# Query scores as two column tiles of 64 and 60 tokens instead of one tile of 120

## The chip, the cores and the metric

The kernel runs on one core of one Trainium2 chip. The metric is the device time of one execution in microseconds (us). Engines: PE is TensorE's matmul, PEld its weight load, DVE VectorE, ACT ScalarE, POOL GpSimd, SP the queue that issues DMAs.

## The reference

Agent attention over 4 batches of 12480 tokens with 128 channels and 49 agents, followed by a feed-forward layer with 2048 hidden units whose activation is h * cos(h). All in float32.

```python
scale = 1 / sqrt(128)
def sm(a, b):                       # softmax over the last axis
    s = scale * (a @ b.transpose(0, 2, 1))
    e = exp(s - s.max(-1, keepdims=True))
    return e / (e.sum(-1, keepdims=True) + 1e-9)
agent_v = sm(agents, k) @ v         # 49 x 128 per batch
x = sm(q, agents) @ agent_v         # 12480 x 128 per batch
h = x @ w_in                        # 128 -> 2048
out = (h * cos(h)) @ w_out          # 2048 -> 128
```

## The kernel before

Tokens go in groups of 960 (GRP): 8 tiles (GT) of 120 tokens (TT), 13 groups a batch, 52 groups in all. The kernel folds `agent_v @ w_in` into one matrix `a` per batch, so that a group's hidden values come straight from its 49 softmax weights per token.

The main loop has 832 steps, 16 for a group: 2 chunks of 480 columns by 8 pairs of hidden blocks. In step n, `first_product` (L976) makes two matmuls into a PSUM tile `ph` (3 buffers), ACT takes the cosine (L979), DVE forms (cos - 1) * h (L985), and four steps later (LAG) `second_product` (L1001) multiplies by `w_out` into a small PSUM tile `one` (2 buffers, of which the output holds one); L997 and L998 add the remaining linear part once a chunk, and ACT copies the chunk out (L1008).

Between these steps stand the pieces that prepare later groups and later batches. They are set to steps by a plan written in the code (`plan`, `early_plan`, `extra`), and a scheduler sets the order of each engine's queue from the program order with a few instructions pinned:

- Query scores of a group (L157, or L167 for the first three groups): for each of the 8 tiles the 120 tokens are the stationary operand (128 channels x 120 tokens) and the 49 agents the moving one. The result has a token in each of 120 PSUM partitions and 8 x 49 columns. These are float32 matmuls, and each stands in the trace as two weight loads and two matmuls: 16 passes a group. ACT or DVE copies the scores to SBUF (L598, L653), DVE takes the maximum (L602), POOL subtracts it (L604).
- The exponentials are not taken group by group but in three windows of the run, in long ACT instructions (L665 for query groups, L497 for the next batch's agents), since ACT must change its table for them (ACT_TABLE_LOAD).
- Weights are normed by POOL (L689) into `p_in`, turned by four transposes (L698) into one PSUM tile, copied by ACT (L702), and split by POOL into `pT` (L705, L706).
- Agent scores of the next batch (L485, L487), their transposes (L505) and their products with the values (L521). L485/L487 and the two kinds of L521 (and L405/L406, L454 in the start-up) already write to partitions 0 to 63 and 64 to 112 of one PSUM tile, as two column tiles.

Before the main loop, a start-up of some 67 us prepares the first batch.

Of the kernel before, what the change touches and what calls it, by code (L numbers as in the profile page):

```python
# [9 lines left out]
F32 = mybir.dt.float32  # L10
# [33 lines left out]
def agent_attention_cos_ffn(ctx, tc, qT, kT, v, vk, vk_rest, agT, w_in, w_out, outT):  # L44
    nc = tc.nc
# [105 lines left out]
    def scores(sb, src, b, ps):  # L151
# [19 lines left out]
    class Weights:  # L171
# [372 lines left out]
    with ExitStack() as pools:  # L544
# [31 lines left out]
        PIECES = 7  # L576

        def piece_tiles(piece):
            e = sb.tile([TT, PIECES * GT, NA], F32, name="e", bufs=3)
            rz = sb.tile([TT, PIECES * GT], F32, name="rz2", bufs=4)  # L580
            for i, k in enumerate(piece):
                e_of[k], rz_of[k] = e[:, i * GT:(i + 1) * GT], rz[:, i * GT:(i + 1) * GT]
                e_of[piece], rz_of[piece] = e[:, :len(piece) * GT], rz[:, :len(piece) * GT]

        def query_parts(n, piece, wide=False, by_vector=False):
            b, g = n // NG, n % NG
            src = qT[b, :, g * GRP:(g + 1) * GRP]
            if wide:
                ps = scores_twice(sb.tile([P, 2 * 512], F32, name="xt", bufs=3)[:, :GRP], src, b, pair())
                yield  # L590
            else:
                ps = scores(sb, src, b, small()).rearrange("p (h t) a -> p h t a", h=2)
# [7 lines left out]
            mx = sb.tile([TT, GT], F32, name="mx2")  # L600
# [3 lines left out]
            on.tensor_sub(e, ps, mx.unsqueeze(3).to_broadcast([TT, 2, HT, NA]))  # L604

        def query_first(n, piece):

            if n == 0:
                e_of["first"] = sb.tile([TT, 3 * GT, NA], F32, name="e", bufs=3)
            e = e_of[n] = e_of["first"][:, n * GT:(n + 1) * GT]  # L610
            rz = rz_of[n] = sb.tile([TT, GT], F32, name="rz2", bufs=4)
            ps = scores_twice(wide_tile()[:, :GRP], qT[0, :, n * GRP:(n + 1) * GRP], 0, pair())
            yield
            mx = sb.tile([TT, GT], F32, name="mx2")
            nc.vector.reduce_max(mx.rearrange("p (h t) -> p h t", h=2), ps, axis=AX.X)
            nc.vector.tensor_scalar(mx, mx, -SC, None, op0=ALU.mult)
            yield
            for t in range(GT):
                nc.scalar.activation(e[:, t], ps[:, t // HT, t % HT], AF.Exp, bias=mx[:, t:t + 1], scale=SC,
                                     accum_out=rz[:, t:t + 1])  # L620
            yield
            nc.vector.tensor_scalar_add(rz, rz, EPS)
            nc.vector.reciprocal(rz, rz)
            yield

        def turned_first():

            p = p_in[0]
            nc.vector.tensor_mul(p.rearrange("p t (h a) -> p h t a", h=2)[:, :, :, :NA],
                                 e_of.pop(0).rearrange("p (h t) a -> p h t a", h=2),  # L630
                                 rz_of.pop(0).rearrange("p (h t) -> p h t", h=2).unsqueeze(3)
                                 .to_broadcast([TT, 2, HT, NA]))
            yield
            pt = small()
            for t in range(HT):
                nc.tensor.transpose(pt[:KR, t * TT:(t + 1) * TT], p[:, t, :KR], ident[:TT, :TT])
            for c, own in enumerate(half_rows):
                nc.scalar.copy(pTs[0][own, c], pt[own, :CH])
            yield
            for c, (own, other) in enumerate((half_rows, half_rows[::-1])):  # L640
                nc.vector.tensor_sub(pTs[0][other, c], pt[own, :CH], pTs[0][own, c].bitcast(F32))

        def query_both(n, piece):

            ps = pair()
            for i in range(2):
                g = (n + i) % NG
                scores(sb, qT[n // NG if n % NG + i < NG else n // NG + 1, :, g * GRP:(g + 1) * GRP], (n + i) // NG, ps[:, i])
# [4 lines left out]
            nc.vector.tensor_copy(e.rearrange("p (i t) a -> p i (t a)", i=2), ps[:TT, :, :GT * NA])  # L653
            mx = sb.tile([TT, 2 * GT], F32, name="mx3")
            nc.vector.reduce_max(mx, e, axis=AX.X)
            for i in range(2):
                part = slice(i * GT, (i + 1) * GT)
                nc.gpsimd.tensor_sub(e[:, part], e[:, part], mx[:, part].unsqueeze(2).to_broadcast([TT, GT, NA]))

        def query(*args):  # L660
            for _ in query_parts(*args):
# [25 lines left out]
        def query_weights(n):  # L687
            e = e_of.pop(n)
            nc.gpsimd.tensor_mul(p_in[n % 2].rearrange("p t (h a) -> p h t a", h=2)[:, :, :, :NA],  # L689
                                 e.rearrange("p (h t) a -> p h t a", h=2),  # L690
                                 rz_of.pop(n).rearrange("p (h t) -> p h t", h=2).unsqueeze(3)
                                 .to_broadcast([TT, 2, HT, NA]))

        def query_turned(n):

            pt = small()
            for t in range(HT):
                mm = nc.tensor.transpose(pt[:KR, t * TT:(t + 1) * TT], p_in[n % 2][:, t, :KR], ident[:TT, :TT])  # L698
                if t in (0,):
                    behind(mm)  # L700
            p = sb.tile([P, CH], F32, name="p", bufs=3)[:KR]
            nc.scalar.copy(p, pt[:KR, :CH])  # L702
            pT = pTs[n % 3]
            for c, (own, other) in enumerate((half_rows, half_rows[::-1])):
                nc.gpsimd.tensor_copy(pT[own, c], p[own])  # L705
# [497 lines left out]
```

## Time and profile before

| | |
|---|---|
| median of 3 runs | 1150.24 us (1149.27 to 1150.82) |
| profiled execution | 1152.38 us, its span 1150.6 us |
| busy in the span | PE 1105.1 us, PEld 845.5, DVE 1038.1, ACT 985.2, POOL 372.8 |
| mean granted clock of TensorE | 0.985 of full speed |
| DMA | 107.70 MB, 94 GB/s in the mean |

The time of a run holds a little more than the span from the first to the last instruction. Matmuls are pipelined: the record of one has its latency in it and overlaps the next one's, so PE's busy share says little by itself, and the distance between the starts of two neighbours says what one costs. A weight load overlaps matmuls in the same way. In rows of the timeline, instructions of one line in a row are merged (x16) and their time runs from the start of the first to the end of the last. "[0.34 <-issue]" is idle time ahead of the row with what ended it.

### The profile page before, as it was taken

How to read it: one execution, taken by the hardware profiler on the slowest of the kernel's cores; microseconds unless marked ns; L12 is line 12 of the kernel's file. 1: busy time of each engine (PE TensorE's matmuls, PEld its weight loads, DVE VectorE, ACT ScalarE, POOL GpSimd, SP SyncE). 2: the span in 40 equal slices, each digit the busy share in tenths (PEclk: the TensorE clock that was granted, in tenths of full speed). 3: DMA queues.
4: the chain of work that ended last, by engine and by line, in shares of the span. 5: the costliest groups of instructions: out<-in, count | busy, mean ns of one | idle time of the engine just before them, and what ended most of it. 6: DMA issues, size and time to landing. Idle time of an engine off the chain costs nothing.

```text
span 1150.6 us, 16640 instructions
## 1 busy us (share of the span) xinstructions
PE 1105.1 (96%) x5879; PEld 845.5 (73%) x5879; DVE 1038.1 (90%) x1156; ACT 985.2 (86%) x1275; POOL 372.8 (32%) x654
## 2 busy tenths in 40 slices
PE   6899999899999999999999999989999999989997
PEld 3676777787877777777886777778787677767775
DVE  5869898789998999989998999989999999999997
ACT  4778777988888998898888989898888899999996
POOL 1021322574132322376222313248413232152320
PEclk9899999999999999989999999999999999989999
DMA  9734445522201234343210232442210000000001
GB/s 363 278 111 125 125 139 178 192 78 81 82 20 61 81 108 142 127 141 109 75 37 35 84 97 88 148 155 72 73 57 19 35 18 35 17 35 18 35 35 38
DMA packets 32509, 107.70 MB, mean 94 GB/s; under 512 B 3617, under 2 KB 4897, under 8 KB 32417
## 3 DMA queue, kind: packets, MB, share of 16 engines
q1 hardware_dynamic: 32416, 106.55, 27.2%
q8 instruction: 49, 0.80, 0.3%
q14 instruction: 44, 0.35, 0.1%
HBM read 80.97 MB, written 25.56 MB: 93 GB/s over the span
## 4 chain that ended last, share of the span: by engine, by line
PE 72%; DVE 16%; ACT 7%; issue 2%; POOL 1%; DMA 0%; SPq 0%; ACTq 0%; DVEq 0%; POOLq 0%
PE ph L976 27%; PE one L1001 24%; DVE r L985 14%; PE one L157 5%; PE one L521 3%; ACT c L979 3%; PE one L485 2%; PE one L998 2%; PE one L997 2%; ACT s L497 1%; PE one L698 1%; PE one L487 1%; PE one L505 1%; PE ph L454 1%; PE one L351 1%
## 5 line engine op out<-in xcount | busy, mean ns | idle before, releaser
L985 DVE SCALAR_TENSOR_TENSOR r<-c,ph 128x960 fp32r<-128x960 f32 x832 | 914.1, 1149 | 56.8 <-ACT c L979 51.6
L979 ACT ACTIVATE c<-ph 128x960 f32<-128x960 f32 x832 | 792.5, 981 | 87.2 <-PE ph L976 68.0
L976 PE MATMUL ph<-pT,a 113*128 113x480 f32 x1664 | 542.8, 405 | 12.3 <-DVE r L985 9.8
L1001 PE MATMUL one<-r,w 128*128 128x480 f32 x1664 | 501.4, 389 | 2.3 <-ACT osb L1008 1.6
L976 PEld LDWEIGHTS ph<-pT,a 113*128 113x128 f32 x1664 | 292.8, 190 | 147.7 <-DVE r L985 85.7
L1001 PEld LDWEIGHTS one<-r,w 128*128 128x128 f32 x1664 | 310.3, 191 | 61.1 <-issue 8.0
L689 POOL TENSOR_TENSOR p<-e,rz 120x392 f32<-120x392 f32 x51 | 43.1, 846 | 331.5 <-PE one L698 307.2
L706 POOL TENSOR_TENSOR pT<-p,pT 49x480 fp32r<-49x480 f32 x102 | 124.1, 1217 | 7.8
L604 POOL TENSOR_TENSOR e<-e,mx 120x392 f32<-120x392 f32 x43 | 36.3, 843 | 218.2 <-DVE mx L602 218.1
L705 POOL CAST pT<-p 49x480 fp32r<-49x480 f32 x102 | 59.4, 583 | 92.4 <-ACT p L702 88.4
L157 PEld LDWEIGHTS one<-ag,xt 128*120 128x120 f32 x688 | 78.8, 185 | 3.0 <-ACT e L598 0.3
L157 PE MATMUL one<-ag,xt 128*120 128x49 f32 x688 | 76.7, 264 | 0.0
L1008 ACT COPY osb<-one 128x480 f32<-128x480 f32 x80 | 44.8, 560 | 2.6 <-PE one L1001 2.6
L676 POOL TENSOR_TENSOR tree<-tree 120x96 f32<-120x96 f32 x132 | 39.9, 302 | 9.9
L598 ACT COPY e<-one 120x392 f32<-120x392 f32 x37 | 18.0, 487 | 27.7 <-PE one L157 27.7
L485 PE MATMUL one<-xt,agp 128*64 128x512 f32 (+1 forms) x78 | 39.7, 591 | 1.8 <-DVE tops L489 1.7
L521 PEld LDWEIGHTS one<-vt,et 128*49 128x49 f32 (+2 forms) x588 | 31.4, 131 | 13.5 <-issue 11.1
L521 PE MATMUL one<-vt,et 128*49 128x128 f32 (+2 forms) x588 | 40.8, 280 | 0.0
L997 PE MATMUL one<-pT,b 113*128 113x480 f32 x104 | 40.6, 390 | 0.0
L998 PE MATMUL one<-pT,b 113*128 113x480 f32 x104 | 40.3, 387 | 0.0
L487 PE MATMUL one<-xt,agp 128*49 128x512 f32 (+1 forms) x78 | 39.3, 585 | 0.0
L602 DVE TENSOR_REDUCE mx<-e 120x8 f32<-120x392 f32 x43 | 24.0, 558 | 10.4 <-ACT e L598 9.3
(149 smaller groups left out, 696.0 us busy)
## 6 DMA issues: line engine op xcount, KB each, us to landing
outT<-osb SPq DMA_DIRECT2D x51, 480.0 KB, 2.5
xt<-qT SPq DMA_DIRECT2D x49, 480.0 KB, 3.6
xt<-kT SPq DMA_DIRECT2D x43, 512.0 KB, 3.6
vt<-vk SPq DMA_DIRECT2D x42, 512.0 KB, 3.9
c<-kT SPq DMA_DIRECT2D x5, 512.0 KB, 6.9
vt<-w_in SPq DMA_DIRECT2D x8, 256.0 KB, 7.1
vt<-w_out SPq DMA_DIRECT2D x8, 256.0 KB, 7.7
c<-vk SPq DMA_DIRECT2D x3, 512.0 KB, 8.9
```

What stands on the lines that cost most here:

```text
L157: mm = nc.tensor.matmul(ps[:, t, :], xt[:, t * TT:(t + 1) * TT], ag[:, b, :], start=True, stop=True)
L485: mm = nc.tensor.matmul(ps[:HI], agp[:, self.b], xt[:, :n], start=True, stop=True)
L487: nc.tensor.matmul(ps[HI:KR], agp[:, self.b, :NA], xt[:, n:], start=True, stop=True)
L521: mm = nc.tensor.matmul(po[h * HI:h * HI + width], e[:, t, h * HI:h * HI + width], vt[:, h * k + t], start=(t == 0), stop=(t == k - 1))
L705: nc.gpsimd.tensor_copy(pT[own, c], p[own])
L706: nc.gpsimd.tensor_sub(pT[other, c], p[own], pT[own, c].bitcast(F32))
L976: nc.tensor.matmul(ph[:, j, :CH], ai[:, f], pTs[q % 3][:, c], start=True, stop=True)
L979: nc.scalar.activation(cos, h, AF.Sin, bias=HALF_PI, scale=1.0)
L985: nc.vector.scalar_tensor_tensor(r, cos, 1.0, h, op0=ALU.subtract, op1=ALU.mult)
L997: nc.tensor.matmul(po, b1[k], pTs[q % 3][:, c], start=False, stop=False)
L998: nc.tensor.matmul(po, b2[k], pTs[q % 3][:, c], start=False, stop=False)
L1001: nc.tensor.matmul(po, w1[:, f, :], r[:, j, :], start=(f == 0), stop=(f == NF - 1))
```

## The change

A tile's 120 tokens are loaded as two stationary operands, tokens 0 to 63 and tokens 60 to 119, which write to PSUM partitions 0 to 63 and 64 to 123. Tokens 60 to 63 of each tile are so computed in both. All tiles that hold a token per partition have 124 rows (QT) instead of 120. The four transposes that turn the weights write 124 columns each at a distance of 128 in PSUM, and the copies out of that tile take 60 (QW) of every 64 columns (`untwined`), so that the 480 columns of `pT` are those of before. In the same way every tile and view with TT rows that holds scores, exponentials or weights of queries (`e`, `rz2`, `mx2`, `mx3`, `tree`, `p_in`) gets QT rows. `scores` stays for the path that the run doesn't take; `query_scores` and `scores_twice` go through the new helper `beside`.

```diff
--- before.py
+++ after.py
@@ -17,7 +17,10 @@
 P = 128
+HI_ROWS = 64
 TT = 120
+QW = 60
+QT = HI_ROWS + QW
 GT = 8
@@ -159,13 +162,32 @@
                 behind(mm)
         return ps
 
+    def beside(xt, t, ag, out):
+
+        for at, lo, n in ((0, 0, HI), (HI, QW, QW)):
+            mm = nc.tensor.matmul(out[at:at + n], xt[:, t * TT + lo:t * TT + lo + n], ag, start=True, stop=True)
+            if t == at == 0:
+                behind(mm)
+
+    def query_scores(sb, src, b, ps):
+
+        xt = sb.tile([P, 2 * 512], F32, name="xt", bufs=3)[:, :GRP]
+        load(xt, src)
+        ps = ps[:QT, :GT * NA].rearrange("p (t a) -> p t a", a=NA)
+        for t in range(GT):
+            beside(xt, t, ag[:, b, :], ps[:, t, :])
+        return ps
+
+    def untwined(pt):
+
+        return pt.rearrange("k (t w) -> k t w", w=HI)[:, :, :QW]
+
     def scores_twice(xt, src, b, ps):
 
         load(xt, src)
-        ps = ps[:TT, :, :HT * 2 * NA].rearrange("p h (t x a) -> p h t x a", x=2, a=NA)
+        ps = ps[:QT, :, :HT * 2 * NA].rearrange("p h (t x a) -> p h t x a", x=2, a=NA)
         for t in range(GT):
-            nc.tensor.matmul(ps[:, t // HT, t % HT], xt[:, t * TT:(t + 1) * TT], twice(ag[:, b, :]),
-                             start=True, stop=True)
+            beside(xt, t, twice(ag[:, b, :]), ps[:, t // HT, t % HT])
         return ps[:, :, :, 0, :]
@@ -563,7 +585,7 @@
         for t in pTs:
             nc.gpsimd.memset(t.bitcast(F32), 0.0)
 
-        p_in = [sb.tile([TT, HT, 2 * HI], F32, name=f"p_{i}", bufs=1) for i in range(2)]
+        p_in = [sb.tile([QT, HT, 2 * HI], F32, name=f"p_{i}", bufs=1) for i in range(2)]
         for t in p_in:
             nc.gpsimd.memset(t, 0.0)
...
             else:
-                ps = scores(sb, src, b, small()).rearrange("p (h t) a -> p h t a", h=2)
+                ps = query_scores(sb, src, b, small()).rearrange("p (h t) a -> p h t a", h=2)
...
         def query_turned(n):
 
             pt = small()
             for t in range(HT):
-                mm = nc.tensor.transpose(pt[:KR, t * TT:(t + 1) * TT], p_in[n % 2][:, t, :KR], ident[:TT, :TT])
+                mm = nc.tensor.transpose(pt[:KR, t * P:t * P + QT], p_in[n % 2][:, t, :KR], ident[:QT, :QT])
                 if t in (0,):
                     behind(mm)
             p = sb.tile([P, CH], F32, name="p", bufs=3)[:KR]
-            nc.scalar.copy(p, pt[:KR, :CH])
+            nc.scalar.copy(p.rearrange("k (t w) -> k t w", w=QW), untwined(pt[:KR]))
             pT = pTs[n % 3]
             for c, (own, other) in enumerate((half_rows, half_rows[::-1])):
                 nc.gpsimd.tensor_copy(pT[own, c], p[own])
```

On PE, this stands around one block of query scores early in the main loop. Before (L976 first products, L1001 second products, L157 the scores):

```order
188 L1001 MATMUL one<-r,w_78 128x480 x4
189 L976 MATMUL ph<-pT_98,a_92 128x480 x2
190 L157 MATMUL one<-ag,xt 120x49 x8
191 L976 MATMUL ph<-pT_99,a_92 128x480 x2
192 L1001 MATMUL one<-r,w_78 128x480 x4
```

After (L999 first products, L1024 second products, L168 the scores; the two score rows stand eight times in turn):

```order
292 L1024 MATMUL one<-r,w_78 128x480 x3
293 L999 MATMUL ph<-pT_98,a_92 128x480 x2
294 L168 MATMUL one<-ag,xt 64x49
295 L168 MATMUL one<-ag,xt 60x49
...
310 L1024 MATMUL one<-r,w_78 128x480
311 L999 MATMUL ph<-pT_99,a_92 128x480 x2
312 L1024 MATMUL one<-r,w_78 128x480 x3
```

Eight matmuls become sixteen in eight pairs, and one second product that stood ahead of the block now stands behind it. A few rows on, where a block stands among second products, nothing but the block itself differs. Before:

```order
234 L1001 MATMUL one<-r,w_78 128x480
235 L157 MATMUL one<-ag,xt 120x49 x8
236 L1001 MATMUL one<-r,w_78 128x480
237 L976 MATMUL ph<-pT_100,a_92 128x480 x2
```

After, on the same engine at the same place:

```order
354 L1024 MATMUL one<-r,w_78 128x480
355 L168 MATMUL one<-ag,xt 64x49
356 L168 MATMUL one<-ag,xt 60x49
...
371 L1024 MATMUL one<-r,w_78 128x480
372 L999 MATMUL ph<-pT_100,a_92 128x480 x2
```

The block keeps its neighbours on both sides. Over the whole run, the blocks of scores, transposes and values stand after the same number of first products as before, and after the same number of second products or one fewer or more; DVE and POOL keep their order, ACT has one pair and SP one pair of neighbours exchanged.

## Rows read from the trace of the kernel before

**Rows 1.** The page: busy us, share of the span and instructions of each engine.
```profile
PE 1105.1 (96%) x5879; PEld 845.5 (73%) x5879; DVE 1038.1 (90%) x1156; ACT 985.2 (86%) x1275; POOL 372.8 (32%) x654
```

**Rows 2.** The chain that ended last: whole run, one block, 67 to 210, 360 to 480.
```profile
by line: PE ph L976 27.4%; PE one L1001 24.1%; DVE r L985 14.3%; PE one L157 5.1%; PE one L521 3.3%; ACT c L979 2.8%; issue 2.3%; PE one L485 1.6%; PE one L998 1.5%; PE one L997 1.5%; ACT s L497 1.5%; PE one L698 1.4%; PE one L487 1.2%; PE 
...
311.94 1.62 PE one L157 x16
...
by line: PE ph L976 25.8%; PE one L1001 25.7%; PE one L157 19.4%; DVE r L985 6.2%; PE one L485 3.8%; issue 3.1%; ACT c L979 2.9%; PE one L487 2.8%; PE one L998 1.5%; PE one L698 1.4%; PE one L997 1.4%; ACT e L665 1.3%; DVE rz L668 0.7%; ACT
...
by line: PE ph L976 35.8%; PE one L1001 31.9%; PE one L157 8.1%; PE one L485 5.0%; DVE r L985 4.7%; PE one L487 3.6%; ACT c L979 2.5%; PE one L997 2.4%; PE one L998 2.4%; PE one L698 2.1%; issue 1.1%; DVE tops L493 0.5%; ACT osb L1008 0.2%;
```

**Rows 3.** Groups on PE, shapes apart: busy us, mean ns of one, idle before.
```profile
L157 PE MATMUL one<-ag,xt 128*120 128x49 f32 x688 | 76.7, 264 | 0.0
...
L157 PE MATMUL ph<-ag,xt 128*120 128x49 f32 x96 | 10.4, 266 | 0.0
```

**Rows 4.** Busy time by stretch: length, PE, PEld, DVE, ACT, POOL, clock, DMA.
```profile
67.00:210.00 143.00, 139.50 (x766) 108.29 (x765) 125.07 (x142) 116.28 (x146) 41.02 (x49) 1.00 0.45 139
225.00:245.00 20.00, 19.36 (x99) 15.92 (x99) 16.22 (x17) 16.67 (x21) 15.39 (x42) 0.83 0.16 58
360.00:480.00 120.00, 119.72 (x585) 90.97 (x584) 115.37 (x114) 107.16 (x134) 31.71 (x36) 1.00 0.37 117
890.00:1010.00 120.00, 119.09 (x501) 86.09 (x501) 117.40 (x115) 112.59 (x144) 29.63 (x35) 1.00 0.08 29
```

**Rows 5.** Timeline (start us, us, what): ordinary matmuls, then a score block's loads.
```profile
304.02 1.04 PE L1001 MATMUL one<-r,w 128*128 128x480 f32 x4
...
311.56 1.87 PEld L157 LDWEIGHTS one<-ag,xt 128*120 128x120 f32 x16
...
313.69 0.19 PEld L1001 LDWEIGHTS one<-r,w 128*128 128x128 f32 x1
```

**Rows 6.** Timeline: 96-column matmuls in two column tiles, L485 and L487.
```profile
201.50 0.13 PEld L485 LDWEIGHTS one<-xt,agp 128*64 128x64 f32 x1 [0.34 <-ACT e L598]
201.51 0.30 PE L485 MATMUL one<-xt,agp 128*64 128x96 f32 x1
201.51 0.17 PEld L487 LDWEIGHTS one<-xt,agp 128*49 128x49 f32 x2
201.51 0.37 PE L487 MATMUL one<-xt,agp 128*49 128x96 f32 x2
201.56 0.14 PEld L485 LDWEIGHTS one<-xt,agp 128*64 128x64 f32 x1
...
201.64 0.25 PE L485 MATMUL one<-xt,agp 128*64 128x96 f32 x1
```

**Rows 7.** Timeline: a values block in two column tiles, and its neighbours.
```profile
301.25 0.38 PE L976 MATMUL ph<-pT,a 113*128 113x480 f32 x1
...
301.56 0.85 PEld L521 LDWEIGHTS one<-vt,et 128*64 128x64 f32 x16 [0.34 <-issue]
...
302.92 0.19 PEld L1001 LDWEIGHTS one<-r,w 128*128 128x128 f32 x1
```

**Rows 8.** Waits of DVE from 67 to 210, then 360 to 480: us, times, longest.
```profile
DVE r L985 <- ACT c L979: 8.9, 21, 1.3
DVE mx L602 <- ACT e L598: 7.6, 8, 1.4
...
DVE r L985 <- ACT c L979: 3.9, 18, 0.6
```

**Rows 9.** Timeline at the end of the first exponential window.
```profile
222.80 0.61 PE L505 MATMUL one<-ident,s 113*128 113x113 f32 x4 [1.91 <-ACT s L497]
...
226.69 1.00 PE L1001 MATMUL one<-r,w 128*128 128x480 f32 x2
```

**Rows 10.** L436 from 52.0 us: ns min/median/max, first and last start in us.
```profile
L436 PE MATMUL one<-ident,s x4: 260/260/316, 53.0 to 53.4; 113*128 113x113 f32 x4
L436 PEldq EVENT_SEMAPHORE  x1: 51/51/51, 52.1 to 52.1; - x1
```

More of the change, by code (lines that the diff above doesn't have):

```diff
@@ L578, in piece_tiles @@
         def piece_tiles(piece):
-            e = sb.tile([TT, PIECES * GT, NA], F32, name="e", bufs=3)
-            rz = sb.tile([TT, PIECES * GT], F32, name="rz2", bufs=4)
+            e = sb.tile([QT, PIECES * GT, NA], F32, name="e", bufs=3)
+            rz = sb.tile([QT, PIECES * GT], F32, name="rz2", bufs=4)
             for i, k in enumerate(piece):
@@ L599, in query_parts @@
                 ps = e
-            mx = sb.tile([TT, GT], F32, name="mx2")
+            mx = sb.tile([QT, GT], F32, name="mx2")
             mx = mx.rearrange("p (h t) -> p h t", h=2)
@@ L603, in query_parts @@
             on = nc.vector if wide else nc.gpsimd
-            on.tensor_sub(e, ps, mx.unsqueeze(3).to_broadcast([TT, 2, HT, NA]))
+            on.tensor_sub(e, ps, mx.unsqueeze(3).to_broadcast([QT, 2, HT, NA]))
         def query_first(n, piece):
             if n == 0:
-                e_of["first"] = sb.tile([TT, 3 * GT, NA], F32, name="e", bufs=3)
+                e_of["first"] = sb.tile([QT, 3 * GT, NA], F32, name="e", bufs=3)
             e = e_of[n] = e_of["first"][:, n * GT:(n + 1) * GT]
-            rz = rz_of[n] = sb.tile([TT, GT], F32, name="rz2", bufs=4)
+            rz = rz_of[n] = sb.tile([QT, GT], F32, name="rz2", bufs=4)
             ps = scores_twice(wide_tile()[:, :GRP], qT[0, :, n * GRP:(n + 1) * GRP], 0, pair())
             yield
-            mx = sb.tile([TT, GT], F32, name="mx2")
+            mx = sb.tile([QT, GT], F32, name="mx2")
             nc.vector.reduce_max(mx.rearrange("p (h t) -> p h t", h=2), ps, axis=AX.X)
@@ L635, in turned_first @@
             for t in range(HT):
-                nc.tensor.transpose(pt[:KR, t * TT:(t + 1) * TT], p[:, t, :KR], ident[:TT, :TT])
+                nc.tensor.transpose(pt[:KR, t * P:t * P + QT], p[:, t, :KR], ident[:QT, :QT])
             for c, own in enumerate(half_rows):
-                nc.scalar.copy(pTs[0][own, c], pt[own, :CH])
+                nc.scalar.copy(pTs[0][own, c].rearrange("k (t w) -> k t w", w=QW), untwined(pt[own]))
             yield
             for c, (own, other) in enumerate((half_rows, half_rows[::-1])):
-                nc.vector.tensor_sub(pTs[0][other, c], pt[own, :CH], pTs[0][own, c].bitcast(F32))
+                nc.vector.tensor_sub(pTs[0][other, c].rearrange("k (t w) -> k t w", w=QW), untwined(pt[own]),
+                                     pTs[0][own, c].bitcast(F32).rearrange("k (t w) -> k t w", w=QW))
         def query_both(n, piece):
@@ L647, in query_both @@
                 g = (n + i) % NG
-                scores(sb, qT[n // NG if n % NG + i < NG else n // NG + 1, :, g * GRP:(g + 1) * GRP], (n + i) // NG, ps[:, i])
+                query_scores(sb, qT[n // NG if n % NG + i < NG else n // NG + 1, :, g * GRP:(g + 1) * GRP], (n + i) // NG, ps[:, i])
             if n == piece[0]:
@@ L652, in query_both @@
             e = e_of[piece][:, i * GT:(i + 2) * GT]
-            nc.vector.tensor_copy(e.rearrange("p (i t) a -> p i (t a)", i=2), ps[:TT, :, :GT * NA])
-            mx = sb.tile([TT, 2 * GT], F32, name="mx3")
+            nc.vector.tensor_copy(e.rearrange("p (i t) a -> p i (t a)", i=2), ps[:QT, :, :GT * NA])
+            mx = sb.tile([QT, 2 * GT], F32, name="mx3")
             nc.vector.reduce_max(mx, e, axis=AX.X)
@@ L672, in query_sum @@
             e, rz = e_of[n], rz_of[n].unsqueeze(2)
-            t = sb.tile([TT, GT, 24], F32, name="tree", bufs=1)
+            t = sb.tile([QT, GT, 24], F32, name="tree", bufs=1)
             src, w = e, 24
```

8 lines of the change are left out of this document (4 added, 4 removed).

## The prediction

> **What bounds the kernel now.** I read the busy table first, then the chain of waits, then both cut by stretch, then single blocks of the timeline. The busy table has PE at 96% and VectorE (DVE) at 90% of the span [rows 1]. That alone names no bound, since matmul records overlap their neighbours. The chain says more: by line it is mostly PE's, and 5.1% of the span, 0.051 x 1150.6 = 58.7 us, is L157, the query scores; one score block of 16 records has 1.62 us on it [rows 2], so about 58.7 / 1.62 = 36 blocks lie on it. There are 688 + 96 records at L157 [rows 3], 784 / 16 = 49 groups; 43 write a small tile and stand alone, 6 write the wide tile `ph` and stand in twos: 46 blocks.
>
> The stretches differ. From 67 to 210 us L157 is 19.4% of the chain, 27.7 us or 17 blocks. From 360 to 480 us it is 8.1%, 9.7 us or 6 blocks [rows 2], and the stretch from 640 to 755 us repeats that one. In the first, DVE is busy 125.07 of 143 us; in the second 115.37 of 120 [rows 4]. So a faster PE has room to pay in the first and little in the second, where DVE is nearly full already. From 890 to 1010 us, with no query scores at all, DVE is busy 117.40 of 120 us [rows 4]: 2.6 us of idle time is what DVE keeps even without these blocks.
>
> **The cost of one block, before.** A weight load (PEld) in the steady stream begins about 3 ns after the matmul ahead of it, so load starts date matmul starts. The first load of the block at 311.56 marks the last ordinary matmul, the load at 313.69 the second ordinary matmul after the block [rows 5]: 2.13 us. Ordinary 480-column matmuls follow each other in (1.04 - 0.38) / 3 = 0.22 us (four records take 1.04 us, one takes 0.38) [rows 5, 7]. The block itself therefore costs 2.13 - 2 x 0.22 = 1.69 us, 0.105 us for each of its 16 passes. A pass streams only 49 columns, so what sets it is the load of 120 weight columns: 0.105 / 120 = 0.88 ns a column.
>
> **The cost of one block, after.** Each tile becomes two matmuls, 64 and 60 weight columns, in two column tiles, both streaming 49 columns: 32 loads and 32 matmuls a group, in 16 pairs. The kernel already has such pairs, which is why this can be priced from its own rows.
> - Do the two of a pair run together? At L485/L487 the loads of 64 and 49 columns begin at 201.50 and 201.51, and the matmuls at 201.51 both [rows 6]. Yes.
> - Is the next load hidden behind the matmul in the same column tile? The second 64-column load begins at 201.56, 0.055 us after the first (that is what a 64-column load takes), and the second 96-column matmul begins at 201.64, 0.08 us after 201.56 [rows 6]. 0.08 / 96 = 0.83 ns a column is the stream of the first matmul alone. Load and stream one after the other would have been 0.055 + 0.08 = 0.135 us. So the load is hidden, and a pair pass costs the longer of the two.
> - What does it cost to go into and out of column tiles? The values block at L521 has 8 pair passes of 128 columns, 8 x 128 x 0.83 ns = 0.85 us. From the last ordinary matmul before it (301.25) to the load at 302.92 are 1.67 us, less 0.44 is 1.23 us [rows 7]. So 0.38 us are the switch; the row itself has 0.34 us of idle time ahead.
>
> In the new block the longer of load (64 columns, 0.055 us) and stream (49 x 0.83 = 0.041 us) is the load; I take 0.056 us. The block is 16 x 0.056 + 0.38 = 1.28 us against 1.69: 0.41 us less.
>
> Bounds for what no row shows, a pair pass this short: below, the stream alone, 0.041 us, block 1.04 us, 0.65 us saved; above, load and stream in sequence, 0.096 us, block 1.92 us, 0.23 us lost. I stay with 0.056 because the hiding itself is shown [rows 6].
>
> The Trainium skill speaks against the change here. "TensorE: Matmul & The Clock Gate", section "Part 3: Packing small matmuls — row/col tiling", says that a weight load overlaps running matmuls only when its row group differs, and column tiles share all rows. By that rule the new block would be 1.92 us. The trace disagrees: 0.08 us where the rule needs 0.135. "TensorEngine Tiling (Array Packing)", section "Key Properties", says that a change of tiling mode drains TensorE; there the trace agrees, with 0.38 us. By the drain alone the gain of a block falls from 0.79 to 0.41 us.
>
> **The other edits.** The three first groups (L167) stream each tile's 49 agents twice, 98 columns, and get 16 x 98 x 0.83 ns = 1.30 + 0.38 = 1.68 us: nothing gained. Four tokens are computed twice, so tiles have 124 rows instead of 120; ACT, DVE and POOL work on the same free sizes, which price their instructions, so I take 0 for them. The copies from PSUM now read 60 of every 64 columns: same 480 elements, 0 by the same reason; if such a read cost 0.1 us it would be 51 x 0.1 = 5 us of ACT, mostly beside PE. The turning transposes stream 124 columns instead of 120: 51 x 4 x 4 x 0.83 ns = 0.7 us, of which I take 0.5. The order on the engines is the old one but for an occasional second-product matmul that now stands behind a block instead of ahead of it, an osb copy on ACT behind one cosine more, and one value load on SP ahead of a query load: 0.
>
> **What of it reaches the end.**
> - 67 to 210 us: 17 blocks x 0.41 = 7.0 us. DVE waited there 8.9 us for cosines and 7.6 us for the copy of the scores [rows 8], so there is something to give. I take all of it.
> - 360 to 480 and 640 to 755 us: 12 blocks, 4.9 us by PE. But DVE's idle 4.6 us in 120 can fall to 2.6, and its wait for cosines there is 3.9 us in all [rows 8]. I take 1.5 us each, 3.0; late next is DVE.
> - The other 36 - 17 - 12 = 7 blocks: 2.9 us.
> - The blocks inside the three exponential windows: 0. There PE ends early and waits 1.91 us for ACT's exponential [rows 9]; it would only wait longer.
>
> 7.0 + 3.0 + 2.9 - 0.5 = 12.4 us. The profiled execution took 1152.38 us (span 1150.6 and 1.8 around it); that is 2.1 above the median of the runs, 1150.24. From the median: 1150.24 - 12.4 = 1137.8, so **1138 us**.
>
> **Rivals.**
> 1. *The loads are not hidden after all in a pass that short*, or the sequencer cannot feed four records in 0.056 us. Price: 36 x 0.23 = 8 us slower, 1158 us. The break-even is a pass of (1.69 - 0.38) / 16 = 0.082 us. For it: the densest steady stream shown, L521, has four records in 128 x 0.83 = 0.106 us; at that rate a block would be 16 x 0.106 + 0.38 = 2.08 us and the kernel 36 x 0.39 = 14 us slower, 1164. Against: the wait instruction ahead of four L436 transposes was done at 52.1 us, and the first of them began only at 53.0 [rows 10]; between the two lies a whole L454 block of 32 records, which the sequencer had passed 0.9 us ahead of the array. Chance 0.11.
> 2. *DVE takes over everywhere.* DVE is at 125 of 143 us even in the best stretch, and its instructions follow one another in order; then only half of the first stretch and of the rest is paid: 3.5 + 0.5 + 0.5 = 4.5 us, 1146 us, between 1143 and 1150. For it: DVE's 90% over the whole span [rows 1]. Against: its waits of 8.9 + 7.6 = 16.5 us in the first stretch [rows 8]. Chance 0.22.
> 3. *PE's whole saving arrives*, all 36 chain blocks and a share of the others with a shorter pass (0.05 us): 36 x 0.5 = 18, and 2 to 4 us of later waits that fall away: 1130 us. Against: DVE's 4.6 us of idle time in the full stretches. Chance 0.12.
> 4. *TensorE's clock.* In the windows PE stands idle, and the granted clock from 225 to 245 us is 0.83 [rows 4], a mix of 2.4 and 1.2 GHz, which makes the low level 20 x 0.17 x 2 = 6.8 us long; two L1001 matmuls take 1.00 us there [rows 9], where four take 1.04 at the high level [rows 5]; (1.00 - 0.60) = 0.40 us from one start to the next, if one record takes 0.60. Shorter score blocks leave PE idler just before. If each of the three windows had half as long again at the low level, 3.4 us, at 4 x 0.40 = 1.6 us of PE a step instead of 4 x 0.22 = 0.88, that would be at most 3.4 x 0.72 / 1.6 = 1.5 us each, 4.6 us: 1142 us. It moves the forecast, not its sign, and has no chance of its own.
>
> **How the numbers follow.** The forecast, 1132 to 1143 us, has 0.55; rivals 1, 2 and 3 have 0.11, 0.22 and 0.12. About 0.2%, 2.3 us, is what a measurement of this kernel can tell from no change. Rival 2 is faster by more than that in about six cases of ten and the same in the rest: faster 0.55 + 0.12 + 0.13 = 0.80, same 0.09, slower 0.11. The range leaves out rival 1 and the ends of rival 3: 1128 to 1150 us.
>
> **What would show it.** Right: pair passes of L168 about 0.056 us apart; 0.3 to 0.4 us of idle weight-load time ahead of each block; 1.2 to 1.3 us a block from ordinary matmul to ordinary matmul; ACT's wait for the scores shorter by 0.4 us a block; most of the gain between 67 and 210 us; DVE's share up by about one point. Wrong: passes of 0.08 us or more; a gain that PE has and the span hasn't; copies by ACT (L598, the copies of turned weights) longer than before; longer low-clock stretches behind the windows.

## The result and the profile after

The changed kernel takes 1135.32 us (median of 4 runs, 1133.65 to 1136.76), the kernel before 1149.98 us beside it: a ratio of 0.9872 (95% interval 0.9855 to 0.9889), 14.7 us less. A second set of runs (`e8_after_again` below) gave 1134.48 us and 0.9851 (0.983 to 0.9872). The forecast was 1138 us, in a range of 1128 to 1150. The profiled execution took 1136.24 us, its span 1134.4, which is 16.2 us shorter than the span before.

The page's busy line after, which answers to [rows 1]:

```profile
PE 1080.5 (95%) x6711; PEld 807.7 (71%) x6711; DVE 1035.0 (91%) x1156; ACT 985.1 (87%) x1275; POOL 372.7 (33%) x654
```

PE has 832 instructions more and 24.6 us less to do, its weight loads (PEld) 37.8 us less; the work of the other engines is the same to about 3 us. The code has moved down by 11 to 23 lines: L157 is now L168, L976 and L979 are L999 and L1002, L985 is L1008, L1001 is L1024, L598 and L602 are L620 and L624.

One score block and its neighbours on TensorE's timeline (start us, us, instruction), to be read as [rows 5] were:

```profile
75.35 0.38 PE L999 MATMUL ph<-pT,a 113*128 113x480 f32 x1
75.65 1.01 PEld L168 LDWEIGHTS one<-ag,xt 128*64 128x64 f32 x32 [0.34 <-issue]
75.66 1.13 PE L168 MATMUL one<-ag,xt 128*64 128x49 f32 x32
...
77.04 0.41 PEld L999 LDWEIGHTS ph<-pT,a 113*128 113x128 f32 x2
```

The last ordinary matmul starts at 75.35, and the load at 77.04 marks the second ordinary matmul after the block: 1.69 us, less 2 x 0.22 is 1.25 us. Measured in the same way for all 43 single blocks the median is 1.256 us, and 1.685 us before: 0.43 us saved a block. Ahead of the block stand the 0.34 us of idle weight-load time that [rows 7] had shown for the other column tiles; (1.25 - 0.34) / 16 = 0.057 us is one pair pass.

The chain that ended last after, by line: whole run, 70 to 206 us, 351 to 469 us (these two hold the work of the stretches of [rows 2]):

```profile
by line: PE ph L999 25.3%; PE one L1024 22.0%; DVE r L1008 18.8%; ACT c L1002 3.6%; PE one L543 3.2%; PE one L168 3.0%; issue 3.0%; PE one L1020 1.5%; PE one L1021 1.5%; ACT s L519 1.5%; PE one L527 1.5%; DMA vt<-w_in 1.4%; PE one L507 1.4%
...
by line: PE ph L999 29.1%; PE one L1024 28.0%; PE one L168 12.5%; DVE r L1008 6.6%; PE one L507 4.4%; PE one L509 3.2%; ACT c L1002 2.8%; issue 2.3%; PE one L1020 1.8%; PE one L1021 1.7%; PE one L721 1.4%; ACT e L688 1.4%; ACT osb L1031 0.8
...
by line: PE ph L999 26.9%; PE one L1024 22.9%; DVE r L1008 19.6%; ACT c L1002 6.0%; PE one L168 4.5%; issue 4.1%; PE one L507 3.6%; PE one L509 2.6%; PE one L1020 2.2%; PE one L1021 2.2%; DVE tops L515 2.0%; PE one L721 1.8%; ACT osb L1031 
```

The scores fall from 5.1% of the chain to 3.0%. In the early stretch DVE's share hardly moves (6.2% before, 6.6% now): TensorE is still what ends last there. In the quiet stretch it goes from 4.7% to 19.6%: there the chain has begun to run through DVE.

Busy time of the same two stretches (start:end, length, PE, PEld, DVE, ACT, POOL, clock, DMA share, GB/s), against [rows 4]:

```profile
70.00:206.00 136.00, 132.23 (x1056) 95.55 (x1051) 125.88 (x147) 116.72 (x147) 42.73 (x51) 1.00 0.46 147
351.00:469.00 118.00, 117.48 (x682) 87.07 (x682) 114.96 (x116) 108.17 (x134) 31.72 (x36) 1.00 0.38 119
```

DVE's idle time is 10.1 of 136 us early (17.9 of 143 before) and 3.0 of 118 us in the quiet stretch (4.6 of 120 before). Its waits in the two stretches (us in all, times, longest), against [rows 8]:

```profile
DVE r L1008 <- ACT c L1002: 6.1, 18, 0.9
DVE mx L624 <- ACT e L620: 3.4, 7, 0.8
...
DVE r L1008 <- ACT c L1002: 2.6, 14, 0.4
```

Where the 16.2 us came from is read by comparing, in both traces, when DVE's product of main-loop step n starts (L985, L1008). "Again" is the trace of `e8_after_again`. The prediction's terms go by stretches of time and not by steps. Of its twelve blocks in the quiet stretches, 0.25 us each, ten stand in steps 208 to 304 and 416 to 512, and two (at 364 and 639 us) in the stretches ahead of these. Four of its seven other blocks stand in these too. The last three stand at the end of the windows' steps, behind the exponential, where the chain of before has them:

```profile
240.07 1.62 PE one L157 x16
...
514.69 1.62 PE one L157 x16
...
789.13 1.62 PE one L157 x16
```

| part of the run | saved | again | predicted |
|---|---|---|---|
| start-up, to step 0 (67.3 us before) | -2.2 | -0.6 | 0 |
| steps 0 to 96 (to 212.8 us before), 18 blocks | 8.6 | 8.5 | 7.0 |
| steps 208 to 304 and 416 to 512 (370 to 489 and 645 to 763 us before), 5 blocks each | 1.8 + 1.9 | 1.8 + 1.9 | 2.5 in all |
| steps 112 to 208 and 320 to 416, 3 blocks each | 1.5 + 1.5 | 1.4 + 1.5 | 2.1 in all |
| the three windows (16 steps each from 96, 304, 512) | 1.0 + 0.6 + 0.4 | 1.6 + 0.8 - 0.5 | 1.2 in all |
| the rest, without query scores | 1.2 | -0.2 | 0 |

The last column, less 0.5 us for the transposes, is the forecast's 12.4 but for rounding. Outside the windows the 34 blocks brought 15.2 and 15.1 us, 0.45 us each: about the 0.43 that each got shorter. Each window holds three single blocks and a double one; two of the single ones and the double one stand ahead of the exponential. There PE's wait for it (us in all, times, longest) grew; before, then after:

```profile
PE one L505 <- ACT s L497: 5.7, 3, 1.9
...
PE one L527 <- ACT s L519: 12.3, 3, 4.1
```

These nine blocks got 6 x 0.43 + 3 x 1.18 = 6.1 us shorter (a double block took 3.366 us before and takes 2.188 after), and 6.6 us more are waited.

### The profile page after: what moved, and what is told of

Its sections match the earlier page's. It is cut to its first block, busy times and chain, and to the rows that moved or that the text cites. A ratio compares the mean times of both kernels' runs of the same rounds, so it can differ in the third digit from the quotient of the medians.

```text
span 1134.4 us, 18304 instructions
## 1 busy us (share of the span) xinstructions
PE 1080.5 (95%) x6711; PEld 807.7 (71%) x6711; DVE 1035.0 (91%) x1156; ACT 985.1 (87%) x1275; POOL 372.7 (33%) x654
## 4 chain that ended last, share of the span: by engine, by line
PE 66%; DVE 20%; ACT 7%; issue 3%; DMA 2%; POOL 1%; SPq 0%; ACTq 0%; DVEq 0%; POOLq 0%
PE ph L999 25%; PE one L1024 22%; DVE r L1008 19%; ACT c L1002 4%; PE one L543 3%; PE one L168 3%; PE one L1020 2%; PE one L1021 2%; ACT s L519 1%; PE one L527 1%; DMA vt<-w_in 1%; PE one L507 1%; PE one L721 1%; PE ph L476 1%; PE one L509 1%
## 5 line engine op out<-in xcount | busy, mean ns | idle before, releaser
L1008 DVE SCALAR_TENSOR_TENSOR r<-c,ph 128x960 fp32r<-128x960 f32 x832 | 913.2, 1148 | 46.6 <-ACT c L1002 42.4
L1002 ACT ACTIVATE c<-ph 128x960 f32<-128x960 f32 x832 | 793.2, 981 | 88.9 <-PE ph L999 66.4
L999 PE MATMUL ph<-pT,a 113*128 113x480 f32 x1664 | 540.8, 404 | 11.6 <-DVE r L1008 8.3
L1024 PE MATMUL one<-r,w 128*128 128x480 f32 x1664 | 502.0, 389 | 2.0 <-ACT osb L1031 1.5
L999 PEld LDWEIGHTS ph<-pT,a 113*128 113x128 f32 x1664 | 293.2, 190 | 145.0 <-DVE r L1008 82.2
L1024 PEld LDWEIGHTS one<-r,w 128*128 128x128 f32 x1664 | 310.1, 190 | 62.6 <-issue 8.8
L712 POOL TENSOR_TENSOR p<-e,rz 124x392 f32<-124x392 f32 x51 | 43.1, 846 | 322.8 <-PE one L721 299.5
L626 POOL TENSOR_TENSOR e<-e,mx 124x392 f32<-124x392 f32 x43 | 36.3, 844 | 211.6 <-DVE mx L624 211.5
L168 PEld LDWEIGHTS one<-ag,xt 128*60 128x60 f32 (+1 forms) x1376 | 43.3, 136 | 14.4 <-issue 10.4
L168 PE MATMUL one<-ag,xt 128*60 128x49 f32 (+1 forms) x1376 | 48.8, 222 | 0.0
L699 POOL TENSOR_TENSOR tree<-tree 124x96 f32<-124x96 f32 x132 | 39.9, 302 | 9.9
L527 PE MATMUL one<-ident,s 113*128 113x113 f32 (+1 forms) x147 | 23.3, 284 | 14.4 <-ACT s L519 12.3
L725 ACT COPY p<-one 113x480 f32<-113x480 f32 x51 | 28.6, 561 | 4.3 <-PE one L721 4.2
```

Source lines behind the costliest of these rows:

```text
L168: mm = nc.tensor.matmul(out[at:at + n], xt[:, t * TT + lo:t * TT + lo + n], ag, start=True, stop=True)
L999: nc.tensor.matmul(ph[:, j, :CH], ai[:, f], pTs[q % 3][:, c], start=True, stop=True)
L1002: nc.scalar.activation(cos, h, AF.Sin, bias=HALF_PI, scale=1.0)
L1008: nc.vector.scalar_tensor_tensor(r, cos, 1.0, h, op0=ALU.subtract, op1=ALU.mult)
L1024: nc.tensor.matmul(po, w1[:, f, :], r[:, j, :], start=(f == 0), stop=(f == NF - 1))
```

## Experiments

Each kernel was timed beside the kernel before on the same chip, which took 1151.87 to 1152.89 us there in the median. "Trace" is the difference of the spans of the profiled executions to the 1150.6 us before.

**1. All edits but the column tiles.** One stationary operand of 124 neighbouring tokens for a tile, so rows 60 to 123 hold other tokens than they should.

```diff
-        for at, lo, n in ((0, 0, HI), (HI, QW, QW)):
-            mm = nc.tensor.matmul(out[at:at + n], xt[:, t * TT + lo:t * TT + lo + n], ag, start=True, stop=True)
+        lo = min(t * TT, GRP - QT)
+        mm = nc.tensor.matmul(out[:QT], xt[:, lo:lo + QT], ag, start=True, stop=True)
...
```

> All edits of the change but the column tiles: each tile is one stationary operand of 124 neighbouring tokens (rows 60 to 123 hold other tokens than they should), with 124-row tiles, transposes of 124 columns and the copies that skip four columns. Theory (the column tiles alone make the gain, the rest is free): a score block costs 16 x 0.108 = 1.73 us against 1.69, so 36 x 0.04 = 1.5 us and up to 0.5 us of transposes above before: 1150 to 1153 us. Rival (the strided copies or the new order share in the result): 1140 to 1147, or above 1155 if these edits cost something that the tiles hid.

Measured: 1153.77 us, ratio 1.0033 (1.0009 to 1.0058). The loads of one of its blocks and the next load that dates a matmul:

```profile
73.88 1.92 PEld L168 LDWEIGHTS one<-ag,xt 128*124 128x124 f32 x16
...
76.05 0.41 PEld L999 LDWEIGHTS ph<-pT,a 113*128 113x128 f32 x2
```

2.17 - 0.44 = 1.73 us a block, 0.046 us over the 1.685 of before: 16 loads of 124 columns instead of 120. Times 36 blocks that is 1.7 us; the medians and the traces differ by 1.2 us, the ratio asks for 3.8 (1.0 to 6.7). The median is 0.8 us above the expected 1153. The trace is finer: outside the windows the steps with its 34 blocks take 1.55 us longer in all, and 34 x 0.046 are 1.56. So the 124 rows, the longer transposes, the copies out of 60 of every 64 columns and the slightly different order cost nothing that can be told, and the whole gain is the column tiles'. The windows scatter more: in this kernel, which has no column tiles, the first one is 1.3 us shorter than before and the other two 0.2 and 0.0 longer.

**2. The first three groups left whole.** Column tiles only from group 3 on.

```diff
+def tiled(n):
+    return n > 2
...
+            if tiled(n):
+                beside(xt, t, twice(ag[:, b, :]), ps[:, t // HT, t % HT])
+            else:
+                nc.tensor.matmul(ps[:, t // HT, t % HT], xt[:, t * TT:(t + 1) * TT], twice(ag[:, b, :]),
+                                 start=True, stop=True)
```

> The change without column tiles in the first three groups (start-up). Theory (the step 0 came 2.2 us later because PE was idler in the start-up and its low clock level lasted 10.2 us there instead of 6.8): the low level is 6.8 us again, step 0 near 67.3 us, 1133 us. Rival (the start-up's 2.2 us are chance between executions, from the landing of DMAs): 1135, no different from the change.

Measured: 1134.55 us, ratio 0.9847 (0.9823 to 0.9871). That could have been a gain over the 0.9872 of the changed kernel; experiments 8 and 10 say that it is none.

**3 and 4. Early groups alone, late groups alone.** `return 2 < n <= 20` and `return n > 20` in the same place.

> Column tiles for groups 3 to 20 alone, nearly all of which stand from 67 to 210 us (18 of the 46 blocks of the main loop). Theory (the gain depends on DVE's room: 8.5 us of the change's gain lie there): 1141 to 1142 us. Rival (every block pays the same share, 14.7 x 18 / 46 = 5.8): 1144 us.

> Column tiles for groups 21 to 51 alone, where DVE is 96% busy in the dense stretches. Theory (DVE's room): 5.5 to 6.5 us of gain, 1143.5 to 1144.5 us. Rival (equal share, 14.7 x 28 / 46 = 8.9): 1141 us.

Measured: early alone 1143.48 us, ratio 0.9925 (0.9904 to 0.9947); late alone 1144.04 us, 0.9927 (0.9905 to 0.9949). By the ratios these are 8.6 and 8.4 us, together 17.0, what the whole change brings (14.7 to 17.4 us by medians). In the traces the early kernel saves 8.5 us between steps 0 and 96, 0.9 in the window behind and 0.2 from there to step 512; the late one saves nothing (0.0) up to step 96 and 9.2 after it. So 18 early blocks are worth 0.47 us each, more than the 0.43 that each got shorter. The late 25 single blocks and 3 double ones got 25 x 0.43 + 3 x 1.18 = 14.3 us shorter; 6.1 of that stand ahead of an exponential, and of the other 8.2 all arrived (9.2, with the scatter of the windows in it). The times expected were meant beside a before of 1150 us, and it took 1152.54 here, so the gains are compared. The theory of DVE's room fits the early kernel (8.5 us expected, 8.6 measured) and not the late one (5.5 to 6.5 expected, 8.4 measured), the equal share fits the late one (8.9) and not the early one (5.8). What fits both is that a block pays its price, early or late, unless it stands ahead of an exponential.

**5. Four column tiles.** 32, 32, 32 and 30 tokens, 126 rows.

```diff
-        for at, lo, n in ((0, 0, HI), (HI, QW, QW)):
+        for at, lo, n in ((0, 0, 32), (32, 30, 32), (64, 60, 32), (96, 90, 30)):
...
```

> Four column tiles of 32, 32, 32 and 30 tokens instead of two (six tokens of a tile computed twice, rows 126). Theory (a pass costs the longer of load and stream): the load of 32 columns takes 0.027 us, the stream of 49 columns 0.041 us, so a pass 0.041 to 0.045 us, a block 1.04 to 1.10 us against 1.26: 0.16 to 0.22 us less; most of 36 blocks of it, 4 to 6 us: 1129 to 1131 us. Rival (the sequencer's feed): the two tiles showed 4 records in 0.057 us; at that 14 ns a record the 8 records of a pass take 0.114 us, a block 2.2 us, 36 x 0.94 = 34 us more: 1169 us; at half of that, 0.057 us, no change from 1135.

Measured: **1127.99 us**, ratio 0.9789 (0.9765 to 0.9813), faster than both kernels, and 1 us below the expected 1129 to 1131. One block:

```profile
74.80 0.38 PE L999 MATMUL ph<-pT,a 113*128 113x480 f32 x1
75.11 0.76 PEld L168 LDWEIGHTS one<-ag,xt 128*32 128x32 f32 x64 [0.34 <-issue]
75.11 0.90 PE L168 MATMUL one<-ag,xt 128*32 128x49 f32 x64
...
76.27 0.41 PEld L999 LDWEIGHTS ph<-pT,a 113*128 113x128 f32 x2
```

1.47 - 0.44 = 1.03 us (median 1.022), with the same 0.34 us ahead. A pass is (1.02 - 0.34) / 16 = 0.043 us, although it has twice as many records as a pass of the change; 49 columns at 0.83 ns [rows 6] are 0.041. That is the longer of load (32 columns) and stream, which was the lower bound of the prediction. At the rate that rival 1 feared (four records in 0.106 us) the eight of this pass would have taken 0.21 us.

**6 and 7. VectorE relieved.** The kernel before and the changed kernel without VectorE's maximum over the query scores of the later groups (zeros are subtracted).

```diff
-            mx = sb.tile([QT, GT], F32, name="mx2")
-            mx = mx.rearrange("p (h t) -> p h t", h=2)
-            nc.vector.reduce_max(mx, ps, axis=AX.X)
+            mx = none[:, :GT].rearrange("p (h t) -> p h t", h=2)
...
```

> The kernel before, with DVE's maximum over the query scores left out (49 groups subtract zeros instead): 26.9 us less work for DVE. Theory (PE bounds the stretches with query scores, DVE is second): little of 26.9 us arrives, 4 to 9 us: 1141 to 1146 us. Rival (DVE is the bound wherever it is over 90% busy): 15 us or more, 1135 us or less.

> The changed kernel with the same maximum left out. Theory (in the later stretches DVE is what the change runs into): the distance to the kernel before with the maximum left out grows from 14.7 to 17 to 20 us. Rival (DVE has nothing to do with the gain's size): the distance stays at 14.7 us.

Measured: 1149.54 us for before, ratio 0.9979 (0.9964 to 0.9994), and 1133.84 us for after, 0.9832 (0.9809 to 0.9856). The busy line of the first, against [rows 1]:

```profile
PE 1102.9 (96%) x5879; PEld 844.2 (74%) x5879; DVE 1013.9 (88%) x1110; ACT 983.4 (86%) x1275; POOL 373.3 (33%) x655
```

And DVE's largest wait over its whole run, which was 51.6 us in the kernel before:

```profile
DVE r L984 <- ACT c L978: 75.8, 133, 1.8
```

24.2 us of DVE's work are gone, 24.2 us more are waited for cosines, and the end moves by 2.4 us, less than the 4 to 9 expected. The amount of DVE's work did not set the time before; nor did it after the change, where the same edit gives 0.6 us against `e8_after_again` by medians and 2.2 us by ratios. The distance from 6 to 7, 15.7 us by medians and 18.2 by traces, is unclear between the two theories' 17 to 20 and 14.7. From 6 to 7 the traces save 8.0 us in steps 0 to 96, 1.2 + 1.2 in the two stretches of 3 blocks and 2.2 + 2.2 in the two quiet stretches of 5: 0.40 to 0.45 us a block everywhere.

**8 to 10. The change again, the windows filled, four tiles with the first groups whole.** 8 is the changed kernel. 9 computes the scores of the double blocks, which lie in the exponential windows, twice. 10 is 5 with the edit of 2.

```diff
-        for t in range(GT):
+        for t in [*range(GT)] * times:
             beside(xt, t, ag[:, b, :], ps[:, t, :])
...
```

> The changed kernel, unaltered, beside the three that follow. If nothing but chance lies between it and the kernel whose first three groups stay whole, its ratio against the kernel before is within 0.003 of that kernel's earlier 0.9847; if the start-up pays for the column tiles of 98 columns, it is below 0.986 only by what the start-up gives. Both theories: 0.985 to 0.989.

> The changed kernel with the scores of the three double blocks, those inside the exponential windows, computed twice over into the same place: 2.1 us more of TensorE work per window, in stretches where TensorE waits for ScalarE's exponentials anyway. Theory A (the clock follows the idle time): the low-clock stretches of the three windows, 10.2, 6.8 and 6.8 us in the changed kernel's profile, shrink by 3 us or more each, and the time falls by 1 to 4 us. Theory B (the windows are set by ScalarE alone): low-clock stretches as they were, PE's wait for the exponential shorter by about 2 us, and the time within 1.5 us of the changed kernel. A third outcome, 4 to 6 us slower, says that window blocks cost their full length, against the prediction's zero for them.

> Four column tiles of 32, 32, 32 and 30 tokens in all groups but the first three, which stay whole. Against four column tiles everywhere (ratio 0.9789): the first three groups work on 98 columns, where a pass is set by the stream of about 0.08 us in either form, so no difference beyond 0.002: ratio 0.977 to 0.981. If the start-up gains from column tiles, it is 0.981 or more.

Measured: 8 1134.48 us, ratio 0.9851 (0.983 to 0.9872); 9 1135.86 us, 0.9862 (0.9841 to 0.9884); 10 1127.90 us, 0.9797 (0.9779 to 0.9816). 8 against 2 and 10 against 5 are each 0.1 us apart: the first three groups gain and lose nothing by column tiles, and the 1.6 us by which the start-up of the two traces of the changed kernel differs (the table above) are chance.

The window shows in 9. First TensorE's timeline at its end in the changed kernel (the bracket is idle time ahead) and the stretches from 215 to 225 us (the granted clock stands after the busy times):

```profile
216.48 1.02 PE L527 MATMUL one<-ident,s 113*128 113x113 f32 x4 [4.10 <-ACT s L519]
```

```profile
215.00:220.00 5.00, 2.80 (x11) 2.31 (x12) 1.26 (x2) 4.97 (x5) 4.53 (x12) 0.50 0.64 253
220.00:225.00 5.00, 5.00 (x19) 3.73 (x19) 4.04 (x4) 4.12 (x6) 4.06 (x15) 0.55 0.25 98
```

Then the same two views of 9:

```profile
216.02 0.60 PE L527 MATMUL one<-ident,s 113*128 113x113 f32 x4 [2.21 <-ACT s L519]
```

```profile
215.00:220.00 5.00, 3.26 (x13) 2.77 (x14) 1.35 (x3) 4.97 (x5) 4.37 (x13) 0.71 0.67 244
220.00:225.00 5.00, 4.63 (x29) 3.13 (x29) 4.66 (x6) 4.31 (x6) 4.35 (x13) 0.95 0.25 101
```

The change lengthened the wait for the exponential from 1.91 us [rows 9] to 4.10, as predicted. With some 2 us of repeated scores in it the wait is 2.21 us, and the transposes right behind it run at 2.4 GHz (0.60 us for four instead of 1.02). The three waits together are 6.6 us, against 12.0 in 8. This window's low stretch is 3.4 us long, against 10.2 in the changed kernel's first trace and 6.8 in its repeat; the other two kept 6.8 each, and the time did not fall. That the repeated scores shortened the low stretch isn't shown: the two traces of the changed kernel differ as much from each other (6.8 and 10.2 us in the third window), and in experiment 1, without column tiles or repeated scores, this window has 3.4 us too. So Theory A's low stretches came in one window of three, perhaps by chance, and its time did not. Theory B's bound of 1.5 us holds (1.4 us slower than 8, intervals overlapping), and so does its shorter wait: a window swallows most of 2 us of extra TensorE work, as it should by the prediction's zero.

**11. A much shorter block.** One matmul of 392 columns on one stationary for a whole group, so that all eight tiles hold the scores of the group's first 124 tokens.

```diff
-        for t in range(GT):
-            beside(xt, t, ag[:, b, :], ps[:, t, :])
+        mm = nc.tensor.matmul(ps, xt[:, :QT], ag[:, b, :].unsqueeze(1).to_broadcast([P, GT, NA]), start=True, stop=True)
+        behind(mm)
```

> The changed kernel with each later group's scores made by one matmul of 392 columns on one stationary of 124 tokens; all eight tiles so hold the scores of the first 124 tokens of their group. An ordinary 480-column pass costs 0.22 us, so a block is 2 x 392 x 0.22 / 480 = 0.36 us instead of 1.256. Theory A (TensorE stays the bound, about 36 blocks on the path): 36 x 0.9 = 32 us less than the changed kernel, 1098 to 1108 us, ratio 0.955 to 0.963. Theory B (VectorE or ScalarE takes over, as the prediction feared for two of its stretches): the gain stops early, 1113 us or more, ratio 0.968 or more, and VectorE's waits for scores and cosines are nearly gone.

Measured: 1123.59 us, ratio 0.9754 (0.9735 to 0.9772). One block on the timeline:

```profile
74.11 0.40 PEld L177 LDWEIGHTS one<-ag,xt 128*124 128x124 f32 x2
74.32 0.82 PE L177 MATMUL one<-ag,xt 128*124 128x392 f32 x2
...
75.20 0.41 PEld L999 LDWEIGHTS ph<-pT,a 113*128 113x128 f32 x2
```

The chain from 68 to 199 and from 342 to 457 us, which hold the work of the early and of the quiet stretch:

```profile
by line: DVE r L1008 22.9%; PE ph L999 20.3%; PE one L1024 16.2%; ACT c L1002 9.8%; issue 4.3%; PE one L177 4.2%; PE one L507 3.4%; DVE mx L624 3.1%; PE one L509 2.4%; ACT e L620 2.1%; DVE tops L515 1.8%; PE one L721 1.6%; ACT e L688 1.4%; 
...
by line: DVE r L1008 39.2%; PE ph L999 18.3%; PE one L1024 14.4%; ACT c L1002 7.0%; issue 4.7%; DVE tops L515 3.1%; PE one L507 2.7%; PE one L509 1.9%; DVE mx L624 1.8%; PE one L1020 1.5%; PE one L1021 1.5%; PE one L721 1.5%; ACT osb L1031 
```

And the busy times there:

```profile
68.00:199.00 131.00, 125.37 (x524) 85.19 (x522) 125.45 (x147) 116.96 (x149) 42.81 (x51) 1.00 0.48 152
342.00:457.00 115.00, 113.78 (x495) 81.70 (x494) 112.86 (x114) 106.08 (x133) 31.76 (x36) 1.00 0.37 121
```

My block price was wrong: 1.09 - 0.44 = 0.65 us (median 0.659), not 0.36. A 392-column pass takes 0.33 us, 0.85 ns a column, the rate of [rows 6], while I had used the 0.46 ns of the 480-column matmuls, whose operands are declared float32r. Put right, Theory A asks for 36 x (1.256 - 0.659) = 21.5 us below the changed kernel; 10.9 came (against 8). DVE's idle time is down to 5.6 of 131 us early and 2.1 of 115 in the quiet stretch, and DVE leads the chain in both. Theory B's time came (1113 us or more), its sign did not: DVE's wait for cosines, 39.2 us over the run, should have been nearly gone, and against 42.4 us in the changed kernel it has hardly changed.

**12. The short block, with VectorE relieved.** The edits of 7 and 11 together.

> The kernel with one matmul of 392 columns a group, once more without VectorE's maximum over the query scores (zeros are subtracted instead; about 23 us of VectorE work less). By its block, 0.66 us against 1.256, it should have been 36 x 0.6 = 21 us below the changed kernel and was 11 us below. Theory (VectorE's amount of work holds back the missing 10 us, since VectorE is 23% of its chain in the early stretch against 7% before): with that work gone most of the missing part comes back, 1113 to 1117 us, ratio 0.966 to 0.970. Rival (not VectorE's amount of work, but ScalarE, or the round trip of matmul, cosine and product from step to step): no more than the same edit gave the kernel before and the changed kernel, 1 to 3 us, so 1120.5 to 1123 us, ratio 0.9725 or more.

Measured: 1117.66 us, ratio 0.9682 (0.9654 to 0.9711). The chain from 68 to 197 us:

```profile
by line: PE ph L998 29.1%; PE one L1023 27.2%; PE one L177 9.5%; ACT c L1001 5.4%; DVE r L1007 5.3%; PE one L507 4.7%; PE one L509 3.4%; issue 3.1%; PE one L720 2.0%; PE one L1019 1.7%; ACT L687 1.7%; ACT e L687 1.4%; PE one L1020 1.4%; PE 
```

The busy times there:

```profile
68.00:197.00 129.00, 125.38 (x529) 87.15 (x527) 119.88 (x133) 117.77 (x150) 43.01 (x51) 1.00 0.48 154
```

The edit that was worth 2.4 us before and 0.6 to 2.2 after is worth 5.9 us here by medians (8.3 by the ratios of the two sets of runs), and DVE's share of the early chain goes from 22.9% back to 5.3%. The ratio lies in the theory's range and below the rival's; the time is 0.7 us over the theory's 1117. Less what the edit gave the changed kernel (0.6 by medians, 2.2 by ratios), DVE's work holds back some 5 to 6 of the 10 us that the short block fails to bring. In steps 0 to 96 the short block saves 14.7 us against before, and 16.9 with VectorE relieved in both (12 against 6), where 18 x 1.03 = 18.5 us of PE's time are gone: more than half of what is missing there comes back. The rest is open.

## Why the prediction was right, point by point

- **The block.** 1.28 us foretold, 1.256 measured; 0.41 us saved foretold, 0.43 measured. Both parts held: the pass is the longer of load and stream with the next load hidden (0.057 us; experiment 5 moves the limit to the stream, 0.043), and the switch costs 0.34 us of idle loading. Rival 1, loads in sequence or a limit of the sequencer, is out: it asked for passes of 0.082 us and more.
- **The other edits at zero.** Right within what can be told (experiment 1). The copy out of 60 of every 64 columns (L702 before, L725 now) did not grow; line, shapes, count, busy us, mean ns:

```profile
L725 ACT COPY p<-one 113x480 f32<-113x480 f32 x51 | 28.6, 561 | 4.3 <-PE one L721 4.2
L721 PE MATMUL one<-ident,p 124*113 124x124 f32 x204 | 30.3, 270 | 0.1
```

It was 562 ns, and the transposes' busy time 29.6 us, before.
- **67 to 210 us, 17 x 0.41 = 7.0 us.** Mis-sized by 1.5: 18 blocks brought 8.5 us, in the change and alone (experiment 3). The mechanism is the one named: DVE's waits for cosines and for the copies fell from 16.5 to 6.1 + 3.4 = 9.5 us, and PE stayed on the chain. ACT's wait for the scores was to be 0.4 us a block shorter; over the run it fell from 27.7 us (37 waits) to 6.0 (11). Why a block brings 0.47 us when PE is 0.43 faster isn't shown.
- **The quiet stretches, 1.5 us each for 6 blocks, 0.25 a block.** The discount was too large: 1.8 to 1.9 us came from 5 blocks in each, 0.37 a block, of 5 x 0.43 = 2.15. The reason given, that DVE's idle time "can fall to 2.6" us, was half right. The direction was: DVE's share of the chain rose there from 4.7% to 19.6%. But 2.6 is no floor (2.1 of 115 us with the short block). With the maximum left out of both kernels all 2.2 us come (experiments 6 and 7), but there the kernel without the change is 0.3 and 0.2 us slower in these stretches than before, so it isn't shown that DVE's work holds back the last 0.3.
- **The seven other blocks, 2.9 us.** The six blocks of steps 112 to 208 and 320 to 416, four of these seven and two of the quiet twelve, brought 3.0 and 2.9 us, 0.5 each where 2.1 in all was foretold. The other three stand in the windows' steps.
- **The blocks inside the windows, 0.** Right: the 6.1 us that they got shorter are in PE's wait for the exponential, which grew by 6.6. The windows' steps as a whole saved 2.0 and 1.9 us, of which the three blocks behind the exponential make 3 x 0.43 = 1.3; the rest is less than the scatter (1.0 us in experiment 1, which has no column tiles).
- **The first three groups, 0.** Right (experiments 8 and 10).
- **The clock, rival 4.** In the three windows together the low stretches are 17.1 us long before and 23.9 in both traces of the changed kernel; the rival had foretold 10.2 us more at most. Whether the change did that is open: experiments 2 and 7, which have its column tiles, show 20.5 us, and so does 6, which has none; 1, which has none either, shows 13.7.
- **Rival 2, DVE takes over everywhere.** Not here: it asked for 4.5 us of gain, and relieving DVE gave 2.4 us before and 0.6 to 2.2 after. It is what comes next, at a block of 0.66 us (experiments 11 and 12).
- **Rival 3, PE's whole saving.** Its mechanism came, at the forecast's block price and without its later waits: 14.7 to 17.4 us by medians, where the forecast had 12.4 and this rival 20 to 22. The 36 chain blocks at 0.43 us are 15.5 us, against 16.2 in both traces. The forecast's own blocks make 36 x 0.41 = 14.8; its range held, but it took off 1.9 us for DVE in the quiet stretches, of which the ten blocks there show some 0.6, and 0.5 for the transposes, of which experiment 1 shows nothing. That both traces sum to 16.2 is chance: start-up and rest make -1.0 in the first and -0.8 in the second out of different parts.

## What to carry over

Price a TensorE block by the distance between the ordinary matmuls on either side of it, take the pass from a block of the same form elsewhere in the kernel, and count only the blocks on the chain: here that gave the block to 0.02 us and the time to 3. That a second engine is 90% busy doesn't yet cap the gain; relieve that engine on its own, and if nothing happens there is still room (four column tiles brought another 6.6 us). The cap shows when the chain's share changes engine, as it did early from 7% to 23% with the shortest block; at 20% in the quiet stretches of the changed kernel a block still paid 0.37 of its 0.43 us. And leave out the blocks ahead of another engine's long instruction: what they save is waited there.

## What the runs showed of the hardware

- The two column tiles of a block don't wait for each other: in the block at 75.65 us the matmuls on 60 columns start 0.055 us apart and those on 64 columns 0.058, so that the last on 60 columns starts at 76.52 and the last on 64, which stands ahead of it in the engine's order, at 76.57.
- Four column tiles take four loads and four matmuls in a pass of 0.043 us, 5 ns a record. The densest stream that the trace of before had shown, four records in 0.106 us [rows 7], was no limit of the sequencer: 27 ns a record.
- Matmuls that the trace calls f32 ran at 0.85 and 0.46 ns a column (392 columns in 0.33 us, 480 in 0.22); the second kind has operands declared float32r.
